# A planner's places, open pairs and initial copies in the projections of a pre-LN transformer block, and the last attention unit's projection in whole rows

## The chip, the cores and the metric

One NeuronCore of a Trainium2 chip runs the whole program; nothing is shared with other cores. The metric is device microseconds of one execution. Engines are named as in the profile: PE is TensorE's matmuls, PEld its weight loads, DVE is VectorE, ACT is ScalarE, POOL is GpSimd, and SP is the engine whose queue issues nearly all DMAs.

## The reference

A sequential block with 2048 tokens of width 640: layer norm without scale, 32-head attention with heads of 20, a residual, layer norm again, a SwiGLU feed-forward of width 1728, a residual.

```python
def _A_ref(x, wqkv, wo):                      # H = 32, Dh = 20
    qkv = transpose((x @ wqkv).reshape(B, S, 3, H, Dh), (2, 0, 3, 1, 4))
    q, k, v = qkv[0], qkv[1], qkv[2]
    p = softmax(einsum("bhqd,bhkd->bhqk", q, k) * Dh ** -0.5)
    o = einsum("bhqk,bhkd->bhqd", p, v)
    return transpose(o, (0, 2, 1, 3)).reshape(B, S, D) @ wo
def _B_ref(x, w_gate, w_up, w_down):
    return (silu(x @ w_gate) * (x @ w_up)) @ w_down
h = x + _A_ref(layernorm(x), wqkv, wo)
return h + _B_ref(layernorm(h), w_gate, w_up, w_down)
```

All in fp32. The kernel keeps the accuracy by splitting an operand into a high part and a rest and adding three products.

## The kernel before

**Stages.** First the projections to queries, keys and values for four chunks of 512 tokens (`query_key`, `value`). Then the attention in 32 units (eight groups of four heads, four query chunks each), each of 16 steps `kt` over 128 keys. Last the output projection, the second norm and the feed-forward; part of the output projection lies inside the last units.

**Two halves of TensorE.** In the projections each product uses 64 of the 128 rows of the array. A job (15 products on the lower half, then 15 on the upper) runs its upper half beside the next job's lower half. `Halves` plans this while the program is written: `t` is the modelled time of each half, `free` that of each engine, `places` the modelled release of each PSUM bank, and `now()`, `use`, `stream` and `wait` move them. The instructions' order on every engine comes out of this model; at run time each engine works through its queue in order and waits on semaphores.

**Pairs.** The softmax needs each query row's maximum over the keys. Part of these maxima is found in the projections, between their products. A *pair* of key blocks is handled as max(a, b) = a + relu(b − a): POOL forms b − a (line 431), one product of the queries with the differences goes through a ReLU on ScalarE into an SBUF place, and a second product with a is added to the place and reduced to a maximum by VectorE, which then releases the place. `max_twice` (lines 217, 231 and 224) does this for one half and leaves the second product as a closure: the pair is *open* until `finish_second` issues it. `max_differences` (lines 194, 205 and 207) does it for both halves at once. `pair` decides whether a pair starts now. There are three places (`relus`: two halves of `spare`, and `third_relu`, given up near the end), and `next_place` hands them out in turn. Before the change at most one pair a half is open:

```python
if half is None and any(self.second) or half is not None and self.second[half]:
    return False
```

**What pairs read.** Keys and queries are written to DRAM by `keep` and loaded back by `stack` (line 161 on SP) into tiles that are free at that time: quarters of `k_stk`, four `raw` tiles in which the weights had arrived, later parts of `xt` and `z_lo`. `raw_place` first copies 1024 finite elements a partition into such a `raw` tile, since POOL's differences run over all 128 rows of it: one copy at job 6, three at job 9 (line 379). `queries_at` is the time from which the planner takes the first units' queries (loaded back the same way) as there.

**Transposes.** The next chunk's normalized tokens are transposed by TensorE in `flip` (line 783), which takes two banks and is copied out by ScalarE (line 791).

**The last units.** A step of a unit issues four scores (line 1374, then the exponential on ScalarE, line 1380) and the weighing of an earlier step's probabilities with the values (`weigh`, line 1384, four matmuls). In the last unit two steps' weighings stand together at even steps and none at odd ones, until `kt` 14 (`both`). Beside them stand the output projection of a chunk (`project`, line 1103: 15 matmuls a product, two products a 128-token tile, eight in all), one a step in steps 0 to 7, and the transposes of its normalized rows (line 1135) in steps 12 to 15. With `halved` a product is split into 30 matmuls of 64 rows in two banks, which VectorE adds one after the other (line 1109); only the projection of chunk 1, inside the last unit, is halved.

Of the kernel before, what the change touches and what calls it, by code (L numbers as in the profile page):

```python
# [13 lines left out]
AF = mybir.ActivationFunctionType  # L14
# [10 lines left out]
NT = S // P  # L25
CH = 512
# [12 lines left out]

LEAST = -3.0e38  # L40
MARGIN = 0.2
BEHIND = 2
SHARE = 4
LAST_QUARTER = 60
# [5 lines left out]
def tile_block(ctx: ExitStack, tc: tile.TileContext, x, wqkv, wo, wg, wu, wd, out):  # L50
# [287 lines left out]
    with tc.tile_pool(name="pa", bufs=2) as pa:  # L338
# [30 lines left out]
        def raw_tile():  # L369
            return pa.tile([P, ND, 2 * P], F32R, name="raw", bufs=4)  # L370

        def raw_place():
            return place(raw_tile().rearrange("p a b -> p (a b)")[:, : 2 * CH], nc.scalar)

        def place(t, engine=nc.sync):

            if engine is nc.scalar:
                some = w_hi.rearrange("p k c -> p (k c)")[:, : 2 * CH].bitcast(F32)
                nc.scalar.activation(t, some, AF.Copy)
                pe.use("scalar", 1.0)  # L380
                return t.rearrange("p (h n) -> p h n", h=2)
            for b in range(2):
                some = w_hi[b * ROW + NPART : (b + 1) * ROW].rearrange("r k c -> r (k c)")[:, : 2 * CH]
                rows = t[b * ROW + NPART : (b + 1) * ROW]
                nc.sync.dma_start(rows.bitcast(F32), some.bitcast(F32))
            pe.sp(n=2, kb=32)
            return t.rearrange("p (h n) -> p h n", h=2)
# [56 lines left out]
        def staged_keys(u, kc, ks, q=None, since=0):  # L444

            ns = ks if q is None else [*ks, q]
            if len(ks) == 2:
                all_products = [
                    (t, pair, b) for t in range(TPC) for pair in range(2) for b in range(2)
                ]  # L450
            else:
                all_products = [(t, pair, None) for t in range(TPC) for pair in range(2)]

            def one(t, pair, b, at):
                rows = queries[u] if q is None else items[q][3]
                if b is None:
                    max_differences(mxs[u], rows, items[ks[0]][3], pair, t, kc, next_place(), at)
                    return over()
                first, more = (items[k][3] for k in ks)
                second = max_twice(mxs[u], rows, first, more, pair, t, kc, b, next_place(), at)  # L460
# [18 lines left out]
            return [  # L479
                (  # L480
                    lambda: slot[0] >= since and all(map(there, ns))
                    and (q is not None or pe.now() >= queries_at.get(u, math.inf)),
                    lambda at, a=a: one(*a, at), a[2],
                )
                for a in all_products
            ]
# [28 lines left out]
        third_relu = v_stk[0].rearrange("p t w -> p (t w)")[:, 2 * CH :]  # L515
        relus.append(third_relu)

        def next_place():
            relus.append(relus.pop(0))
            return relus[-1]  # L520

        def next_pair():
            load_items()
# [6 lines left out]
        class Halves:  # L530
# [5 lines left out]
            def __init__(self):  # L536
                self.t = [0.0, 0.0]
                self.free = dict.fromkeys(("vector", "scalar", "pool", "sync", "dma"), 0.0)
                self.places = dict.fromkeys(range(8), 0.0)
                self.second = [None, None]  # L540
                self.last = 0.0
                self.jobs = []

# [61 lines left out]
            def pair(self):  # L605
                t = self.now()
                if not self.banks(1):
                    return False
                queue = next_pair()
                if queue is None:  # L610
                    return False
                least = int(self.t[1] < self.t[0])
                ahead = 0
                if queue[0][2] == 1 - least and len(queue) > 1 and queue[1][2] == least:
                    ahead = int(queue[1][0]())
                half = queue[ahead][2]
                if half is None and any(self.second) or half is not None and self.second[half]:
                    return False
                at = self.banks(1 if half is not None else 2)
                if at is None:  # L620
                    return False
                second = queue.pop(ahead)[1](at)
                if half is not None:
                    start = self.stream(half, 0.231)
                    seen = self.use("scalar", 0.48, start + 0.43) + 0.2
                    self.places[at[0]] = seen
                    self.second[half] = second, seen
                    return True
                for half in range(2):
                    self.stream(half, 0.231)  # L630
                ends = [t + 0.43] * 2
                ends = [self.use("scalar", 0.3, end) + 0.2 for end in ends]
                for i, end in zip(at, ends):
                    self.places[i] = self.use("vector", 0.36, end) + 0.14
                return True

            def before_flip(self):
# [33 lines left out]
            def finish_second(self, half):  # L671
                if not self.second[half]:
                    return False
                second, seen = self.second[half]
                at = self.banks(1)
                if at is None or self.now() + 0.43 < seen:
                    return False
                self.second[half] = None
                second(at)
                start = self.stream(half, 0.231)  # L680
                self.places[at[0]] = self.use("vector", 0.62, max(seen, start + 0.43)) + 0.14
                return True

            def wait(self, us):
# [148 lines left out]
        def keep(c, m, ps):  # L833

            e = next_e()
            start = max(pe.now() + 0.4, e_free.get(id(e), 0.0))
            if slot[0] < 8:
                done = pe.use("scalar", 0.5, start)
                free = ready = pe.use("vector", 0.62, done + 0.2)
                split(ps, e[:, 0], e[:, 1], nc.vector)  # L840
            else:
                free = pe.use("scalar", 0.5, start)
                done = pe.use("scalar", 0.5)
                engine, ready = pe.second_part(done + 0.2)
# [12 lines left out]
            store(e, ready + 0.2, *pieces)  # L857
            return free
# [73 lines left out]
        for at, (kind, c, *which) in enumerate(work):  # L932
# [55 lines left out]
            for u, when in enumerate((5, begins(1) + 14, begins(2) + 14)):  # L988
                if at == when - 4:
                    es[:] = [e for e in es if all(e is not stored(q) for q in lent[:u])]  # L990
                if at == when:
                    assert landed[0, 0, u] == GD
                    load_queries(u)
                    queries_at[u] = pe.sp(n=4, kb=750) + 3.5
            if 0 in ends:
                finish_at = min(finish_at, at + 2)
                if at == finish_at:
# [457 lines left out]
    for u in range(NU):  # L1455
# [4 lines left out]
        for kt in range(NT):  # L1460
# [5 lines left out]
            for op in order:  # L1466
# [2 lines left out]
                elif op in "sS":  # L1469
                    scores(u, kt, heads[op == "S"].pop(0), probs)  # L1470
                else:
                    both = u == NU - 1 and kt < NT - 1
                    for _ in range(2 * (1 - kt % 2) if both else 1):
                        if todo:
                            weigh_next()
# [58 lines left out]
    def ps_b():  # L1534
        return banks[:, turn(one_places)]
# [554 lines left out]
```

## Time and profile before

| | us |
|---|---|
| median of three runs (lowest, highest) | 2037.76 (2036.97, 2040.04) |
| the profiled execution | 2040.81 |
| its span, first to last instruction | 2039.0 |
| projections, from the start to the first scores | 335 |
| attention up to the last unit | 1089 |
| last unit of the attention | 53 |
| the rest | 563 |

The mean granted TensorE clock is 0.996 of full speed. In the lines of the profile a row of a timeline has the start, the busy time, the engine, the line, the operation with what it writes and reads, the count, and in brackets the idle time of the engine ahead of it with what ended it. A row of a window has its bounds, its length, the busy time and count of PE, PEld, DVE, ACT and POOL, the granted clock, the DMA share and GB/s. Matmuls overlap, so their busy times add to more than the distance of their starts.

### The profile page before, as it was taken

How to read it: one execution, taken by the hardware profiler on the slowest of the kernel's cores; microseconds unless marked ns; L12 is line 12 of the kernel's file. 1: busy time of each engine (PE TensorE's matmuls, PEld its weight loads, DVE VectorE, ACT ScalarE, POOL GpSimd, SP SyncE). 2: the span in 40 equal slices, each digit the busy share in tenths (PEclk: the TensorE clock that was granted, in tenths of full speed). 3: DMA queues.
4: the chain of work that ended last, by engine and by line, in shares of the span. 5: the costliest groups of instructions: out<-in, count | busy, mean ns of one | idle time of the engine just before them, and what ended most of it. 6: DMA issues, size and time to landing. Idle time of an engine off the chain costs nothing.

```text
span 2039.0 us, 39356 instructions
## 1 busy us (share of the span) xinstructions
PE 2009.1 (99%) x13836; PEld 1244.3 (61%) x13836; DVE 1616.7 (79%) x3261; ACT 1463.3 (72%) x2948; POOL 778.5 (38%) x1075
## 2 busy tenths in 40 slices
PE   7999999999999999999999999999999999999998
PEld 6888897333333333333333333345598888888888
DVE  7769776888888888888888888886478666676677
ACT  4887887999999999999999999996634222212221
POOL 4464342234343434344430011001146454754555
PEclk9999999999999999999999999999999999999999
DMA  7775574343533534444433123211159654974642
GB/s 228 236 214 184 167 215 116 104 137 103 150 125 108 158 112 143 135 145 137 149 127 108 30 61 83 82 62 49 36 180 325 208 193 154 350 267 158 204 149 92
DMA packets 205206, 304.93 MB, mean 150 GB/s; under 512 B 47648, under 2 KB 82720, under 8 KB 203984
## 3 DMA queue, kind: packets, MB, share of 16 engines
q1 hardware_dynamic: 204912, 302.40, 45.6%
q8 instruction: 110, 1.80, 0.4%
q14 instruction: 88, 0.72, 0.1%
q10 hardware_dynamic: 96, 0.00, 0.0%
HBM read 205.78 MB, written 95.68 MB: 148 GB/s over the span
## 4 chain that ended last, share of the span: by engine, by line
PE 94%; DMA 2%; DVE 1%; ACT 1%; POOL 1%; issue 1%; SPq 0%; DVEq 0%; ACTq 0%; POOLq 0%
PE banks L1384 25%; PE banks L1374 17%; PE banks L1552 16%; PE banks L238 12%; PE banks L1646 8%; PE banks L569 8%; PE banks L1103 3%; PE banks L217 3%; PE banks L194 1%; DMA qk_d<-e 0%; PE banks L826 0%; PE banks L263 0%; DMA q_stk<-qk_d 0%; ACT q_stk L231 0%; DMA xt<-in_A_x 0%
## 5 line engine op out<-in xcount | busy, mean ns | idle before, releaser
L1380 ACT ACTIVATE probs<-banks 128x512 f32<-128x512 f32 x2048 | 1056.2, 614 | 61.1 <-PE banks L1374 25.3
L244 DVE TENSOR_REDUCE mx<-banks 128x1 f32<-128x512 f32 x1472 | 925.4, 684 | 124.9 <-PE banks L238 76.3
L1374 PE MATMUL banks<-q_stk,k_stk 62*128 62x512 f32 x2048 | 583.2, 428 | 1.5 <-ACT probs L1380 1.5
L1384 PE MATMUL banks<-probs,v_stk 128*32 128x512 f32 x4096 | 545.4, 606 | 0.0
L238 PE MATMUL banks<-k_stk,q_stk 60*128 60x512 f32 x1472 | 486.7, 438 | 0.2
L1374 PEld LDWEIGHTS banks<-q_stk,k_stk 62*128 62x128 f32 x2048 | 291.8, 184 | 283.7 <-ACT probs L1380 271.4
L238 PEld LDWEIGHTS banks<-k_stk,q_stk 60*128 60x128 f32 x1472 | 244.2, 184 | 163.1 <-DVE mx L244 126.8
L1769 DVE TENSOR_TENSOR tmp<-banks,tmp 128x512 f32<-128x512 f32 x208 | 141.2, 689 | 118.4 <-PE banks L1552 92.8
L1384 PEld LDWEIGHTS banks<-probs,v_stk 128*32 128x32 f32 x4096 | 81.3, 108 | 183.1 <-issue 171.4
L1646 PE MATMUL banks<-halves,yp 128*128 128x320 f32 x1032 | 178.9, 308 | 1.4 <-POOL yp L97 1.2
L1646 PEld LDWEIGHTS banks<-halves,yp 128*128 128x128 f32 x1032 | 165.2, 188 | 17.4 <-POOL yp L97 1.5
L1552 PE MATMUL banks<-t,units 128*128 128x512 f32 x624 | 162.7, 396 | 0.1
L97 POOL TENSOR_TENSOR yp<-y,yp 128x256 fp32r<-128x256 f32 x96 | 60.3, 628 | 195.2 <-ACT yp L96 181.0
L1552 PE MATMUL banks<-z,units 128*128 128x512 f32 x516 | 133.8, 394 | 0.0
L255 POOL CAST both<-neg 128x16 fp32r<-128x16 f32 x32 | 6.6, 206 | 314.7 <-PE banks L1374 138.2
L1552 PEld LDWEIGHTS banks<-t,units 128*128 128x128 f32 x624 | 112.5, 188 | 18.9 <-DVE tmp L1769 0.3
L1651 DVE TENSOR_TENSOR h<-banks,h 128x320 f32<-128x320 f32 x248 | 110.0, 481 | 6.8 <-PE banks L1646 5.4
L224 DVE CUSTOM_DVE_ANT_0 q_stk<-banks,q_stk 128x512 f32<-128x512 f32 x139 | 92.7, 687 | 26.0 <-PE banks L217 13.2
L569 PE MATMUL banks<-z_hi,w_hi 64*128 64x512 f32 x380 | 102.4, 406 | 1.9 <-ACT z_hi L96 1.8
L569 PE MATMUL banks<-z_lo,w_hi 64*128 64x512 f32 x380 | 103.3, 395 | 0.0
L1552 PEld LDWEIGHTS banks<-z,units 128*128 128x128 f32 x516 | 93.1, 187 | 16.1 <-DVE tmp L1769 0.2
L96 ACT ACTIVATE yp<-tmp 128x512 fp32r<-128x512 f32 x40 | 25.3, 632 | 103.2 <-POOL tmp L1639 103.2
(213 smaller groups left out, 2960.9 us busy)
## 6 DMA issues: line engine op xcount, KB each, us to landing
units<-w_d SPq DMA_DIRECT2D x186, 256.0 KB
w_d<-stage SPq DMA_DIRECT2D x106, 256.0 KB
halves<-j_d SPq DMA_DIRECT2D x70, 320.0 KB
k_stk<-qk_d SPq DMA_DIRECT2D x116, 160.0 KB
j_d<-stage SPq DMA_DIRECT2D x42, 320.0 KB
q_stk<-qk_d SPq DMA_DIRECT2D x64, 160.0 KB
k_stk<-qk_d SPq DMA_DIRECT2D x116, 80.0 KB
rb<-r_d SPq DMA_DIRECT2D x32, 256.0 KB
```

Of the source, the lines that this page charges most:

```text
L217: nc.tensor.matmul(ps, q[rows, pair, t * P : (t + 1) * P], k[rows, pair, :], start=True, stop=True)
L224: nc.vector.tensor_tensor_reduce(out=place, in0=ps, in1=place, scale=1.0, scalar=LEAST, op0=ALU.add, op1=ALU.max, accum_out=mx[:, b, pair, ...
L238: nc.tensor.matmul(ps, queries[u][rows, pair, t * P : (t + 1) * P], keys[u // NC][rows, pair, kc * CH : (kc + 1) * CH], start=True, stop=True,
L244: nc.vector.tensor_reduce(mxs[u][:, b, pair, t, kc : kc + 1], ps, axis=AX.X, op=ALU.max)
L569: product = nc.tensor.matmul(job["ps"][:, :out], lhs, rhs, start=(half == 0 and i == 0), stop=(half == 1 and i == job["n"] - 1),)
L1374: nc.tensor.matmul(ps, keys[u // NC][rows, p, kt * P : (kt + 1) * P], queries[u][rows, p, :], start=True, stop=True,)
L1380: nc.scalar.activation(probs[p][:, b, :], ps, AF.Exp, scale=scale)
L1384: nc.tensor.matmul(acc[32 * j : 32 * j + 32, :], values[u // NC][:, kt, j * VW : j * VW + 32], probs[j // 2][:, j % 2, :], start=(kt == 0) ...
L1552: nc.tensor.matmul(ps.rearrange("p (t n) -> p t n", t=TPC), w[k][:, i], z[k][:, :, j], start=(first and m == 0), stop=(last and m == len(n ...
L1646: nc.tensor.matmul(ps, a, b, start=(n == 0), stop=(n == len(pairs) - 1))
L1651: nc.vector.tensor_tensor(out=h, in0=ps, in1=h, op=ALU.add)
L1769: add = lambda out, ps, x: nc.vector.tensor_tensor(out=out, in0=ps, in1=x, op=ALU.add)
```

## The change

Seven edits. In the planner: a pair's place is the one with the earliest modelled release (`relu_at`), and a pair starts only if that lies before its ReLU could begin (`free_place`); up to two pairs a half are open (`OPEN`). The initial copies of the `raw` tiles go from ScalarE to VectorE, and `place_at` keeps such a tile unused until the copy's modelled end. In `keep` the modelled times of two ScalarE steps go from 0.5 to 0.62 and 0.54 us. The allowance for the first queries' landing goes from 3.5 to 4.5 us. In the last unit the weighings stand in twos only until `kt` 9. No projection is halved any more.

```diff
+OPEN = 2
-            if engine is nc.scalar:
+            if engine is nc.vector:
                 some = w_hi.rearrange("p k c -> p (k c)")[:, : 2 * CH].bitcast(F32)
-                nc.scalar.activation(t, some, AF.Copy)
-                pe.use("scalar", 1.0)
-                return t.rearrange("p (h n) -> p h n", h=2)
+                nc.vector.tensor_copy(t, some)
+                t = t.rearrange("p (h n) -> p h n", h=2)
+                place_at[id(t)] = pe.use("vector", 0.65) + 0.2
+                return t
...
-        def next_place():
-            relus.append(relus.pop(0))
-            return relus[-1]
+        relu_at = {}
+        def free_place(at):
+            place = min(relus, key=lambda r: relu_at.get(id(r), 0.0))
+            return place if relu_at.get(id(place), 0.0) <= at else None
...
-                if half is None and any(self.second) or half is not None and self.second[half]:
+                if half is None and any(self.second) or half is not None and len(self.second[half]) == OPEN:
                     return False
                 at = self.banks(1 if half is not None else 2)
                 if at is None:
                     return False
-                second = queue.pop(ahead)[1](at)
+                place = free_place(t + 0.43)
+                if place is None:
+                    return False
+                second = queue.pop(ahead)[1](at, place)
+                relu_at[id(place)] = math.inf
...
-                    self.second[half] = second, seen
+                    self.second[half].append((second, seen, place))
...
+                relu_at[id(place)] = self.places[at[1]]          # pair
...
-                self.second[half] = None
+                del self.second[half][0]
                 second(at)
                 start = self.stream(half, 0.231)
                 self.places[at[0]] = self.use("vector", 0.62, max(seen, start + 0.43)) + 0.14
+                relu_at[id(place)] = self.places[at[0]]          # finish_second
...
-                free = pe.use("scalar", 0.5, start)
-                done = pe.use("scalar", 0.5)
+                free = pe.use("scalar", 0.62, start)
+                done = pe.use("scalar", 0.54)
...
-                    queries_at[u] = pe.sp(n=4, kb=750) + 3.5
+                    queries_at[u] = pe.sp(n=4, kb=750) + 4.5
...
-                    both = u == NU - 1 and kt < NT - 1
+                    both = u == NU - 1 and kt < NT // 2 + 2
...
                     ahead = projection(
-                        c - 1, ps_max if c < NC - 1 else (lambda: ps_b()), c == NC - 2
+                        c - 1, ps_max if c < NC - 1 else (lambda: ps_b())
                     )
```

The order of the instructions changes from the first pair on. Line numbers of the new program are 1 to 10 higher (569 is 573, 194 is 195, 783 is 793, 1374 is 1384, 1384 is 1394, 1103 is 1113, 1135 is 1145).

TensorE at the first pair of the projections (L783 is the first transpose, L569 a projection's product, L194 the first pair's two products). Before:

```order
L783 MATMUL banks<-ident,xt 128x64 x8
L569 MATMUL banks<-z_lo,w_hi 128x512
L194 MATMUL banks<-k_stk_116,q_stk 128x512 x2
L569 MATMUL banks<-z_hi,w_hi 128x512
L569 MATMUL banks<-z_lo,w_hi 128x512
```

Now:

```order
L793 MATMUL banks<-ident,xt 128x64 x8
L573 MATMUL banks<-z_lo,w_hi 128x512
L573 MATMUL banks<-z_hi,w_hi 128x512
L573 MATMUL banks<-z_lo,w_hi 128x512
L573 MATMUL banks<-z_hi,w_hi 128x512
L573 MATMUL banks<-z_lo,w_hi 128x512
L573 MATMUL banks<-z_hi,w_hi 128x512
L573 MATMUL banks<-z_lo,w_hi 128x512
L573 MATMUL banks<-z_hi,w_hi 128x512
L573 MATMUL banks<-z_lo,w_hi 128x512
L195 MATMUL banks<-k_stk_116,q_stk 128x512 x2
```

Eight more products of a projection stand ahead of the first pair.

ScalarE around the three copies of job 9 before (L791 and L96 belong to a transpose, L205 are ReLUs of pairs):

```order
L791 ACTIVATE xt<-banks 128x4x64 x2
L96 ACTIVATE z_hi<-xt 128x512
L379 ACTIVATE raw<-w_hi 128x1024 x3
L205 ACTIVATE v_stk_117<-banks 128x256 x2
L205 ACTIVATE q_stk<-banks 128x256 x4
```

VectorE there now (ISA is the reduction of a pair with its accumulator read, L98 a rest of a split):

```order
L208 ISA v_stk_117,mx_121<-banks,v_stk_117 128x256
L208 ISA mx_121 128x1
L380 CAST raw<-w_hi 128x1024 x3
L98 TENSOR_TENSOR v_stk_117<-v_stk_117 128x512
L208 ISA q_stk,mx_121<-banks,q_stk 128x256
```

The copies left ScalarE's queue ahead of the ReLUs and stand in VectorE's between two pairs' reductions.

TensorE in the last unit from step 11 on (L1374 scores, L1384 weighings of four matmuls a step, L1135 transposes, L1103 the projection that follows). Before:

```order
L1374 MATMUL banks<-q_stk,k_stk_4721 128x512 x8
L1384 MATMUL banks<-probs,v_stk_4722 32x512 x8
L1135 MATMUL banks<-ident,z_17209 128x128 x5
L1374 MATMUL banks<-q_stk,k_stk_4721 128x512 x4
L1135 MATMUL banks<-ident,z_17239 128x128 x5
L1374 MATMUL banks<-q_stk,k_stk_4721 128x512 x4
L1384 MATMUL banks<-probs,v_stk_4722 32x512 x8
L1135 MATMUL banks<-ident,z_17264 128x128 x5
L1374 MATMUL banks<-q_stk,k_stk_4721 128x512 x4
L1384 MATMUL banks<-probs,v_stk_4722 32x512 x4
L1135 MATMUL banks<-ident,z_17293 128x128 x5
L1384 MATMUL banks<-probs,v_stk_4722 32x512 x4
```

Now, from step 13 on:

```order
L1394 MATMUL banks<-probs,v_stk_4722 32x512 x4
L1145 MATMUL banks<-ident,z_17107 128x128 x5
L1384 MATMUL banks<-q_stk,k_stk_4721 128x512 x4
L1394 MATMUL banks<-probs,v_stk_4722 32x512 x4
L1145 MATMUL banks<-ident,z_17136 128x128 x5
L1384 MATMUL banks<-q_stk,k_stk_4721 128x512 x4
L1394 MATMUL banks<-probs,v_stk_4722 32x512 x4
L1145 MATMUL banks<-ident,z_17161 128x128 x5
L1394 MATMUL banks<-probs,v_stk_4722 32x512 x8
L1113 MATMUL banks<-wo_hi,o_hi 128x320 x5
```

Each step now has its scores, one weighing and one transpose, and two weighings in place of one stand at the end.

More of the change, by code (lines that the diff above doesn't have):

```diff
@@ L372, in raw_place @@
         def raw_place():
[L373 removed]
+            return place(raw_tile().rearrange("p a b -> p (a b)")[:, : 2 * CH], nc.vector)
         def place(t, engine=nc.sync):
[L377 removed]
+            if engine is nc.vector:
                 some = w_hi.rearrange("p k c -> p (k c)")[:, : 2 * CH].bitcast(F32)
[L379 to L381 removed]
+                nc.vector.tensor_copy(t, some)
+                t = t.rearrange("p (h n) -> p h n", h=2)
+                place_at[id(t)] = pe.use("vector", 0.65) + 0.2
+                return t
             for b in range(2):
@@ L452, in staged_keys, with one @@
                 all_products = [(t, pair, None) for t in range(TPC) for pair in range(2)]
-            def one(t, pair, b, at):
+            def one(t, pair, b, at, place):
                 rows = queries[u] if q is None else items[q][3]
                 if b is None:
-                    max_differences(mxs[u], rows, items[ks[0]][3], pair, t, kc, next_place(), at)
+                    max_differences(mxs[u], rows, items[ks[0]][3], pair, t, kc, place, at)
                     return over()
                 first, more = (items[k][3] for k in ks)
-                second = max_twice(mxs[u], rows, first, more, pair, t, kc, b, next_place(), at)
+                second = max_twice(mxs[u], rows, first, more, pair, t, kc, b, place, at)
                 return lambda at: (second(at), over())
@@ L482, in staged_keys @@
                     and (q is not None or pe.now() >= queries_at.get(u, math.inf)),
-                    lambda at, a=a: one(*a, at), a[2],
+                    lambda at, place, a=a: one(*a, at, place), a[2],
                 )
@@ L539, in __init__ @@
                 self.places = dict.fromkeys(range(8), 0.0)
-                self.second = [None, None]
+                self.second = [], []
                 self.last = 0.0
@@ L673, in finish_second @@
                     return False
-                second, seen = self.second[half]
+                second, seen, place = self.second[half][0]
                 at = self.banks(1)
```

## The prediction

> **What bounds the kernel now.** I read the page first, then the stages, then TensorE's waits in the stages that the change touches.
>
> ```profile
> PE 2009.1 (99%) x13836; PEld 1244.3 (61%) x13836; DVE 1616.7 (79%) x3261; ACT 1463.3 (72%) x2948; POOL 778.5 (38%) x1075
> PE 94%; DMA 2%; DVE 1%; ACT 1%; POOL 1%; issue 1%; SPq 0%; DVEq 0%; ACTq 0%; POOLq 0%
> 0.00:335.00 335.00, 314.30 (x2856) 289.05 (x2857) 246.81 (x864) 252.19 (x545) 150.33 (x126) 0.98 0.66 204
> 1423.80:1476.40 52.60, 51.55 (x453) 31.09 (x449) 23.66 (x59) 34.97 (x68) 7.51 (x5) 0.97 0.12 35
> ```
>
> The first line is the busy time of each engine, the second the chain that ended last by engine, and the other two are stages: length, then busy time of PE, PEld, DVE, ACT and POOL, the granted clock, the DMA share and GB/s. TensorE is the chain, so the time moves only if its idle time, its clock or its own work moves. The change touches two stages. The projections (0 to 335 us) keep TensorE busy 314.3 of 335 us at a clock of 0.98. The last unit of the attention (1423.8 to 1476.4 us) is its end.
>
> What TensorE waits for between 17 and 335 us (waiter, releaser, us, times, longest), and below it two waits of ACT that lie behind the largest of them:
>
> ```profile
> PE banks L217 <- ACT q_stk L231: 4.3, 5, 1.6
> PE banks L783 <- DVE mx L207: 1.7, 1, 1.7
> PE banks L194 <- DMA q_stk<-qk_d: 1.3, 2, 1.0
> PE banks L217 <- ACT v_stk L231: 1.2, 1, 1.2
> PE banks L194 <- DMA raw<-qk_d: 0.5, 1, 0.5
> PE banks L783 <- ACT q_stk L231: 0.4, 1, 0.4
> ...
> ACT q_stk L231 <- DVE mx L224: 7.0, 6, 2.0
> ACT v_stk L231 <- DVE mx L224: 2.0, 2, 1.3
> ```
>
> A pair product waits because its bank still waits for ScalarE's ReLU. That ReLU waits because the place it writes is still being read by VectorE's reduction. This is 4.3 + 1.2 + 0.4 = 5.9 us of TensorE, from 9.0 us of ScalarE.
>
> A wait costs more than itself. The granted clock stood at half in four stretches (the seventh column of figures, 0.50):
>
> ```profile
> 46.94:50.35 3.41, 3.41 (x18) 3.09 (x20) 2.75 (x9) 1.99 (x6) 0.58 (x1) 0.50 0.59 179
> 60.59:64.00 3.41, 3.37 (x23) 3.28 (x25) 1.57 (x9) 3.35 (x10) 1.65 (x2) 0.50 0.59 210
> 173.23:176.64 3.41, 3.41 (x20) 3.16 (x18) 3.04 (x13) 1.72 (x4) 0.00 (x0) 0.50 0.31 118
> 1463.47:1466.88 3.41, 3.41 (x20) 1.12 (x13) 0.00 (x0) 1.56 (x3) 1.54 (x1) 0.50 0.02 5
> ```
>
> Each lasts 3.41 us and does half the work, so it costs 1.7 us; three stand behind a wait in the projections and one in the last unit. The Trainium skill, "TensorE: Matmul & The Clock Gate", Part 1, says that TensorE's clock is halved after an idle window of about 3.4 us on a free-running grid. The length agrees with these rows; the windows ahead of them were not wholly idle, so here a part of a window is enough.
>
> **The change part by part.** The profiled execution took 2040.8 us (span 2039.0), 3.0 us above the median 2037.8 of the three runs. The sum is made against 2040.8, and its difference is then taken from the median.
>
> *First pair (the queries' allowance 3.5 to 4.5).* In the new order nine products of a projection stand ahead of the first pair, where one stood.
>
> ```profile
> 26.26 1.29 PE L569 MATMUL banks<-z_lo,w_hi 64*128 64x512 f32 x5
> 28.98 0.98 PE L569 MATMUL banks<-z_hi,w_lo 64*128 64x512 f32 x6
> 29.66 0.39 PE L569 MATMUL banks<-z_lo,w_hi 64*128 64x512 f32 x1
> 46.00 0.47 PE L194 MATMUL banks<-k_stk,q_stk 60*128 60x512 f32 x1 [1.03 <-DMA q_stk<-qk_d]
> 46.79 0.63 PE L194 MATMUL banks<-k_stk,q_stk 60*128 60x512 f32 x1 [0.32 <-DMA q_stk<-qk_d]
> ```
>
> One product takes 0.39 us; six that alternate between the halves take 0.98, so they start (0.98 − 0.39) / 5 = 0.12 us apart; five of one half take 1.29, so 0.23 apart. Eight products earlier fill 8 × 0.12 = 0.9 us of the wait, which the landings (46.00 and 46.79) set and which doesn't move. The half-clock stretch at 46.94 then has a busier window ahead; I give its going 0.7. Term: −0.9 − 0.7 × 1.7 = −2.1 us (0 to −2.6).
>
> *Initial copies into the four places, ScalarE to VectorE.*
>
> ```profile
> 56.56 2.93 ACT L379 ACTIVATE raw<-w_hi 128x1024 fp32r<-128x1024 f32 x3
> 59.79 0.42 DVE L207 CUSTOM_DVE_ANT_0 v_stk<-banks,v_stk 128x256 f32<-128x256 f32 x1 [5.30 <-ACT v_stk L205]
> L755 DVE TENSOR_SCALAR xt<-xt,mv,r_a x8: 605/610/1587, 11.1 to 41.7; 128x640 f32<-128x640 f32 x8
> 52.32 0.42 DVE L207 CUSTOM_DVE_ANT_0 v_stk<-banks,v_stk 128x256 f32<-128x256 f32 x1 [2.31 <-ACT v_stk L205]
> ```
>
> Three copies hold ScalarE for 2.93 us; VectorE sits idle 5.30 us behind them, and TensorE's transposes (L783) 1.65 us behind VectorE, then run at half clock. With the copies on VectorE, ScalarE's ReLUs start 2.9 us earlier. No row shows such a copy on VectorE; the nearest one-operand row does 640 elements in 0.605 to 1.587 us, so 1024 cost some 0.6 us at least and 2.5 at most, 2 to 7.5 us for the three. I take about 1 each, near the median row. Cover: VectorE's idle 2.31 and 5.30 us at that place. Without cover they delay three pairs' reductions, and the 1.65 us stays. The fourth, at about 38 us, stands ahead of the normalization that feeds the first transposes; what it delays is made up by the wait for the queries behind. Term: −0.8 × (1.65 + 1.7) = −2.7 us (0 to −3.4).
>
> *Places by modelled release, two open pairs a half.* A pair now starts only when a place is free in the model, so part of the 9.0 us of ScalarE's waits becomes projection products put ahead. But the model's release is no measurement, and the place is taken as soon as it says so. I take a third of 5.9 + 1.7 = 7.6 us, −2.5 (0 to −7.6, and the other sign as a rival). Against it, pairs bunch on one half: counted over the order by operand rows, products that follow one of their own half rise from 474 to 514. Each gives up at most 0.23 − 0.12 = 0.11 us: 40 × 0.11 = 4.4 us if TensorE would otherwise not have waited. I take +3.0 (0 to +4.4), since most of the stage is not waiting. In the new order the last pairs stand at the end of the projections, not some jobs ahead of it; their loads move with them on SP, and POOL's differences behind those. Apart from the queries TensorE waited for such a load once, 0.5 us; I take 0, and 2 at most, four such waits. The allowances of 0.62 and 0.54 us issue nothing: 0.
>
> *Weighing in the last unit (paired until step 10, not 15).*
>
> ```profile
> L1380 ACT ACTIVATE probs<-banks 128x512 f32<-128x512 f32 x32 | 16.2, 622 | 6.5 <-PE banks L1374 5.8 <-PE banks L1103 0.8
> 1467.65 4.03 ACT L1380 ACTIVATE probs<-banks 128x512 f32<-128x512 f32 x8 [2.62 <-PE banks L1374]
> 1458.01 1.92 PE L1384 MATMUL banks<-probs,v_stk 128*32 128x512 f32 x16
> 1459.86 0.73 PE L1374 MATMUL banks<-q_stk,k_stk 62*128 62x512 f32 x4
> 1473.41 1.06 PE L1384 MATMUL banks<-probs,v_stk 128*32 128x512 f32 x8
> 1474.41 0.77 PE L1135 MATMUL banks<-ident,z 128*128 128x128 f32 x5
> 1476.38 1.00 PE L1103 MATMUL banks<-wo_hi,o_hi 128*128 128x320 f32 x5
> ```
>
> The first row is ScalarE between 1452 and 1476.4 us: eight steps of exponentials, 16.2 / 8 = 2.03 us a step, and 5.8 us idle until scores. A double weighing holds TensorE 1.85 us (1458.01 to 1459.86) ahead of the next scores, with a flip 2.6 us, more than ScalarE's 2.03. A single one holds it 1.0 us, with a flip (0.77) 1.8, so ScalarE is then nearly fed. I leave 1.5 us of the 5.8 for the four flips, whose banks VectorE must empty, and 1.0 us for the one weighing that now comes behind the last exponential: −(5.8 − 1.5 − 1.0) = −3.3 us (−0.5 to −4.8). The half-clock stretch at 1463 lies inside these 5.8 us and isn't counted again. What follows at 1476.38 is TensorE's own work, so the gain stays.
>
> *Whole rows for the second projection (eight products of 15 matmuls).*
>
> ```profile
> 1366.27 1.00 PE L1103 MATMUL banks<-wo_hi,o_hi 128*128 128x320 f32 x5
> 1367.10 0.90 PE L1103 MATMUL banks<-wo_lo,o_hi 128*128 128x320 f32 x5
> 1367.84 0.90 PE L1103 MATMUL banks<-wo_hi,o_lo 128*128 128x320 f32 x5
> 1368.66 0.50 PE L1374 MATMUL banks<-q_stk,k_stk 62*128 62x512 f32 x1
> 1423.88 1.03 PE L1103 MATMUL banks<-wo_hi,o_hi 64*128 64x320 f32 x10
> 1426.20 0.63 PE L1374 MATMUL banks<-q_stk,k_stk 62*128 62x512 f32 x4
> L1103 PEld LDWEIGHTS banks<-wo_lo,o_hi 128*128 128x128 f32 x120 | 18.6, 188 | 0.0
> ```
>
> Whole rows take 1368.66 − 1366.27 = 2.39 us, halves 1426.20 − 1423.88 = 2.32. Eight times 0.07 is +0.6; half of VectorE's adds for it go, off the path. I take +0.3 (−0.6 to +2.5, the upper end if the scores beside it no longer slip in between the halves). The same page of the Trainium skill, Part 3, "The mechanism", says that weight loads overlap running matmuls only in other row groups, which speaks against whole rows. The trace disagrees: five whole products start within 0.74 us (1367.10 to 1367.84), 0.15 each, less than a load's 0.188. By that rule the sum would be the last rival's.
>
> Sum: −2.1 − 2.7 − 2.5 + 3.0 − 3.3 + 0.3 = −7.3 us: 2033.5 us for an execution like the profiled one, 2030.5 for the median.
>
> **The rivals.** *The modelled release is too early (slower).* VectorE's row of 0.605 to 1.587 us shows that equal work varies by 1 us, and the norm's steps sit in front of the reductions. With two pairs open, ScalarE meets an unreleased place more often; all behind it in its queue (the evictions, the flips' copies) waits too, and then TensorE. If the eight waits become sixteen, TensorE pays another 5.9 us and two more half-clock stretches, 3.4: −2.1 − 2.7 + 3.0 − 3.3 + 0.3 + 9.3 = +4.5, or 2042.3 us. It ends above today's time from about fifteen waits on. For it: no slack is added to the modelled release. Against it: the before had no check at all. 0.16.
>
> *The waits only move (no change).* The queries still land at 46.79, the half-clock stretches come back at other places, the flips in the last unit wait for VectorE: −0.9 for the first pair, −1.65 for the transposes, +3.0, −1.0 in the last unit, 0 elsewhere: −0.5, or 2037.3 us. Also the case in which three places keep two open pairs from ever mattering. 0.16.
>
> *Whole rows expose their loads (slower).* 8 × 15 × 0.188 = 22.6 us: −7.6 + 22.6 = +15, or 2052.8 us. The rows above speak against it. 0.03.
>
> **How the numbers follow.** The forecast has 0.65; its own range is 2024 to 2036 us. Best ends of all terms: −2.6 − 3.4 − 7.6 + 0 − 4.8 − 0.6 = −19; unlikely together. The range reaches from 2022 to 2042.5: it takes in the no-change case and the first rival, and leaves out some 0.07 below and 0.1 above. A measurement of this kernel tells about 0.2% (4.1 us) from no change, so faster means under 2033.7 and slower over 2041.8. Faster 0.62 (nearly all of the forecast's 0.65); same 0.20 (the rest of it, the no-change case and the milder first rival); slower 0.18.
>
> **What would show it.** Right: no L783 wait for a reduction near 60 us; no half clock in the first 65 us; ScalarE's waits for mx reductions below 6 us; projections ending some 4 us earlier than 335 us; ScalarE's idle time ahead of exponentials in the last eight steps near 2 us. Wrong: TensorE's waits for ReLUs at 6 us or more, or copies on VectorE over 2 us with the transposes still waiting. Projection products slower than 2.5 us in the last unit would refute the whole-rows term.

## The result and the profile after

The changed kernel took 2030.6 us (median of 8 runs, 2027.9 to 2034.9), the kernel before 2038.6 us (median of 8, 2034.7 to 2040.1): ratio 0.9965, 95% interval 0.9953 to 0.9976, so 8 us or 0.35% faster. The forecast was 2030.5 us. The sum came out; most of its terms, as the experiments show, did not, so that the match is luck.

The profiled execution of the changed kernel took 2031.8 us with a span of 2030.0, 9.0 us less than the one before. Its page, busy time by engine and the chain that ended last:

```profile
PE 2004.5 (99%) x13716; PEld 1237.3 (61%) x13716; DVE 1622.2 (80%) x3257; ACT 1459.9 (72%) x2944; POOL 777.7 (38%) x1075
...
PE 91%; DMA 3%; DVE 2%; POOL 1%; ACT 1%; issue 1%; SPq 0%; ACTq 0%; POOLq 0%; DVEq 0%
```

TensorE is still the bound. The same stages as before (busy time of PE, PEld, DVE, ACT, POOL; the granted clock is the column after POOL's), and the one half-clock stretch that is left before the end:

```profile
0.00:327.90 327.90, 311.08 (x2856) 284.10 (x2857) 254.44 (x868) 248.76 (x541) 148.57 (x126) 1.00 0.67 208
1416.70:1467.50 50.80, 50.35 (x333) 28.47 (x329) 20.55 (x52) 35.00 (x68) 7.56 (x5) 0.97 0.12 35
1452.50:1455.91 3.41, 3.41 (x16) 0.85 (x12) 0.00 (x0) 2.80 (x6) 0.00 (x0) 0.50 0.00 0
```

The projections end 7.1 us earlier (327.9 against 335.0 us, with the same 2856 matmuls), at clock 1.00 in place of 0.98: the three half-clock stretches, 3 x 1.7 = 5.1 us, are absent, TensorE's waits below are 4.1 us shorter (7.9 against 12.0), and what is left, TensorE's own work in its new order, is 2.0 us longer. From there to the last unit the two traces run in step, 7.1 us apart. The last unit is 1.8 us shorter, with one half-clock stretch in it as before.

TensorE's waits between 17 and 320 us (us, times, longest), and below them ScalarE's for reductions:

```profile
PE banks L573 <- ACT z_hi L97: 2.1, 2, 1.2
PE banks L573 <- DVE mx L225: 1.2, 1, 1.2
PE banks L218 <- ACT e L352: 1.1, 1, 1.1
PE banks L218 <- DVE mx L225: 0.8, 1, 0.8
PE banks L836 <- ACT z_hi L97: 0.8, 1, 0.8
PE banks L793 <- DVE mx L208: 0.7, 1, 0.7
PE banks L573 <- DVE mx L208: 0.5, 1, 0.5
PE banks L793 <- DVE xt L765: 0.5, 1, 0.5
PE banks L573 <- ACT ev L883: 0.2, 1, 0.2
...
ACT q_stk L232 <- DVE mx L225: 3.9, 6, 2.2
ACT v_stk L232 <- DVE mx L225: 2.7, 3, 1.7
ACT q_stk L206 <- DVE mx L225: 0.5, 1, 0.5
```

The rows of before that had a ReLU as releaser (L217 and L783 behind L231, 5.9 us) are all gone. ScalarE still waits 7.1 us for reductions, in ten places, against 9.0 in eight, but no row of TensorE's has a ReLU behind such a wait as its releaser any more.

### The profile page after: what moved, and what is told of

It is laid out like the page before. It is cut to its first block, busy times and chain, and to the rows that moved or that the text cites. A ratio compares the mean times of both kernels' runs of the same rounds, so it can differ in the third digit from the quotient of the medians.

```text
span 2030.0 us, 39123 instructions
## 1 busy us (share of the span) xinstructions
PE 2004.5 (99%) x13716; PEld 1237.3 (61%) x13716; DVE 1622.2 (80%) x3257; ACT 1459.9 (72%) x2944; POOL 777.7 (38%) x1075
## 3 DMA queue, kind: packets, MB, share of 16 engines
q8 instruction: 109, 1.79, 0.4%
## 4 chain that ended last, share of the span: by engine, by line
PE 91%; DMA 3%; DVE 2%; POOL 1%; ACT 1%; issue 1%; SPq 0%; ACTq 0%; POOLq 0%; DVEq 0%
PE banks L1394 25%; PE banks L1384 17%; PE banks L1562 16%; PE banks L239 11%; PE banks L1656 8%; PE banks L573 6%; PE banks L1113 4%; PE banks L218 2%; DMA k_stk<-qk_d 1%; PE banks L195 1%; DMA raw<-qk_d 1%; DMA qk_d<-e 1%; PE banks L836 0%; DMA qk_d<-q_stk 0%; DMA v_d<-ev 0%
## 5 line engine op out<-in xcount | busy, mean ns | idle before, releaser
L1390 ACT ACTIVATE probs<-banks 128x512 f32<-128x512 f32 x2048 | 1056.3, 612 | 59.0 <-PE banks L1384 22.6
L1384 PE MATMUL banks<-q_stk,k_stk 62*128 62x512 f32 x2048 | 581.3, 430 | 1.1 <-ACT probs L1390 1.1
L1384 PEld LDWEIGHTS banks<-q_stk,k_stk 62*128 62x128 f32 x2048 | 290.6, 185 | 284.8 <-ACT probs L1390 271.1
L98 POOL TENSOR_TENSOR yp<-y,yp 128x256 fp32r<-128x256 f32 x96 | 60.4, 630 | 195.1 <-ACT yp L97 180.8
L573 PE MATMUL banks<-z_hi,w_lo 64*128 64x512 f32 x380 | 102.0, 391 | 0.0
```

Source lines behind the costliest of these rows:

```text
L573: product = nc.tensor.matmul(job["ps"][:, :out], lhs, rhs, start=(half == 0 and i == 0), stop=(half == 1 and i == job["n"] - 1),)
L1384: nc.tensor.matmul(ps, keys[u // NC][rows, p, kt * P : (kt + 1) * P], queries[u][rows, p, :], start=True, stop=True,)
L1390: nc.scalar.activation(probs[p][:, b, :], ps, AF.Exp, scale=scale)
```

## The experiments

Each was timed in five rounds beside the kernel before; the ratios below are to that. Line numbers are those of the kernel that is changed, give or take one.

**The projections' edits without the last unit's** (from the changed kernel):

```diff
-                    both = u == NU - 1 and kt < NT // 2 + 2
+                    both = u == NU - 1 and kt < NT - 1
...
-                        c - 1, ps_max if c < NC - 1 else (lambda: ps_b())
+                        c - 1, ps_max if c < NC - 1 else (lambda: ps_b()), c == NC - 2
```

> The changed kernel with its two edits in the last unit undone: weighing paired until step 15 and the second projection in halves again, as before; the whole change of the projections stays. By the prediction's terms the projections give -2.1 - 2.7 - 2.5 + 3.0 = -4.3 us (ratio 0.998). Theory from the two traces: the projections end 7.1 us earlier (327.6 against 334.8 us), the three half-clock stretches there (5.1 us) being gone, so -7 us (0.9965). Rival: the whole change comes from the last unit and the profiled projections were a lucky execution: 0 to -2 us.

Measured: 2031.4 us, 0.9961 (0.9947 to 0.9975), as the changed kernel within the intervals. The projections carry the change; their end lies at 326.8 us. The two edits of the last unit add nothing here that the times can tell.

**The weighing alone** (kernel before, `kt < NT // 2 + 2`):

> The kernel before, with the weighing paired until step 10 as the only edit. Prediction: -3.3 us (ratio 0.9984), ScalarE's idle time ahead of exponentials in the last eight steps from 5.8 to some 2 us. Rival: the flips then wait for VectorE, -1.0 us (0.9995). Projections and halves as before: no row outside the last eight steps moves.

Measured: 2035.4 us, 0.9976 (0.9966 to 0.9986), -2.9 to -6.9 us. From the score of step 505 (of 512) to the last weighing it needs 18.4 us, the kernel before 20.9, each with one half-clock stretch there: -2.6 us. Over the other profiles, without a stretch it is 19.3 us paired and 17.3 us single (-2.0). ScalarE's idle time until scores in the last eight steps is 2.4 us in this run, as priced (5.8 before). In the changed kernel, between 1444.5 and 1467.5 us, it is 3.1 us:

```profile
ACT probs L1390 <- PE banks L1384: 3.1, 5, 1.0
```

**Whole rows alone** (kernel before, without `c == NC - 2`):

> The kernel before, with whole rows for the second projection as the only edit. Prediction: +0.3 us (ratio 1.000). Theory from the trace after: two steps of the last unit take 7.98 us in place of 7.75 while the projection runs, four times 0.23, so +0.9 us (1.0005). Rival, weight loads exposed: +15 us (1.007).

Measured: 2039.4 us, 1.0001 (0.9991 to 1.0011): no difference that can be told. Steps 496 to 505 show it nevertheless: 33.8 to 33.9 us in every profile with whole rows, 33.0 in every one with halves, so +0.9. Where it lies is seen in TensorE's timeline (start, length), first before, then after:

```profile
1433.22 0.90 PE L1103 MATMUL banks<-wo_hi,o_lo 64*128 64x320 f32 x10
1433.96 0.63 PE L1374 MATMUL banks<-q_stk,k_stk 62*128 62x512 f32 x4
1434.43 0.46 PE L1103 MATMUL banks<-wo_hi,o_hi 64*128 64x320 f32 x2
```

```profile
1424.72 1.00 PE L1113 MATMUL banks<-wo_hi,o_hi 128*128 128x320 f32 x5
1425.56 0.90 PE L1113 MATMUL banks<-wo_lo,o_hi 128*128 128x320 f32 x5
1426.30 0.90 PE L1113 MATMUL banks<-wo_hi,o_lo 128*128 128x320 f32 x5
1427.12 0.74 PE L1384 MATMUL banks<-q_stk,k_stk 62*128 62x512 f32 x4
1427.79 1.00 PE L1113 MATMUL banks<-wo_hi,o_hi 128*128 128x320 f32 x5
```

The product itself takes 2.40 us (1424.72 to 1427.12), as priced. The four scores behind it cost 0.67 us from start to next start, beside halves 0.47. This meeting comes once in two steps, so four times 0.2, or 0.8 of the 0.9.

**The copies alone** (kernel before, the four copies on VectorE with their price and `place_at`):

> The kernel before, with the four copies on VectorE (priced 0.65 us each in the model, with the time at which the place may be loaded) as the only edit. Prediction: -2.7 us (ratio 0.9987): no wait of a transpose near 60 us, no half-clock stretch behind it. Rival (waits only move): -1.65 us and a half-clock stretch elsewhere, 0 net. The model's prices change, so the order behind the copies changes too; if that order alone matters, the difference may have either sign by 2 us with waits at other places.

Measured: 2043.2 us, 1.0021 (1.0011 to 1.0031): slower. No transpose waits near 60 us and no half-clock stretch lies in the projections, and still they end at 334.6 us. TensorE's waits for ReLUs stand in the new order as in the old:

```profile
PE banks L217 <- ACT q_stk L231: 4.5, 4, 1.4
PE banks L217 <- ACT v_stk L231: 0.6, 1, 0.6
```

**The places undone** (changed kernel; the places in turn, one open pair):

```diff
-            place = min(relus, key=lambda r: relu_at.get(id(r), 0.0))
-            return place if relu_at.get(id(place), 0.0) <= at else None
+            relus.append(relus.pop(0))
+            return relus[-1]
```

> The changed kernel with the part on the places undone: the three places are taken in turn again whatever their release, one open pair a half; all other edits stay. Theory (the release is what removes the waits): TensorE's waits for ReLUs that wait for a reduction, 0 in the changed kernel, come back to 4 to 6 us, with one or two half-clock stretches of 1.7: +5 to +8 us on the changed kernel, 2036 to 2039 us. TensorE's order taken alone (each product as long as its columns, halves side by side) is as long as that of the changed kernel (299.0 against 299.1 us), so the order says 0. Rival (the changed kernel's order is a lucky one and the release does nothing): 2031 us, or any value within 4 us, with no such waits.

Measured: 2036.4 us, 0.9980 (0.9971 to 0.9989). The projections end at 333.4 us, 5.7 later than in the changed kernel, and these waits come back, 6.2 us:

```profile
PE banks L218 <- ACT v_stk L232: 2.9, 2, 1.6
PE banks L218 <- ACT q_stk L232: 2.4, 4, 1.1
PE banks L793 <- ACT q_stk L232: 0.9, 2, 0.6
```

**One open pair a half** (changed kernel, `OPEN = 1`):

> The changed kernel with one open pair a half in place of two; places by modelled release as in the change. Theory: the release alone keeps ReLUs from waiting, and with one open pair fewer products follow one of their own half (490 against 514; TensorE's order taken alone is 297.1 against 299.1 us): -2 us on the changed kernel, 2028.5 us, waits for ReLUs still 0. Rival (the second open pair is what gives the planner enough pairs to put in): pairs fall behind, +2 us or more, 2033 us.

Measured: 2032.4 us, 0.9959 (0.9944 to 0.9973), as the changed kernel within the intervals. The waits are lower still (4.6 us, none for ReLUs), but the pairs fall behind: the projections' last product stands at 317.3 us, and pairs are left with nothing beside them. A half-clock stretch of three times 3.41 us stands there, which costs 5.1 us. The run before this one differs from it only in how a place is chosen: without the check on the release it took 4.0 us more, with 6.2 us of waits for ReLUs against none. The half clock:

```profile
322.79:333.03 10.24, 10.02 (x36) 5.55 (x39) 7.56 (x30) 8.47 (x21) 7.01 (x2) 0.50 0.18 50
```

**Copies back on ScalarE** (changed kernel):

> The changed kernel with the four copies on ScalarE again. Prediction's term: +2.7 us, 2033.3 us, with a transpose waiting for a reduction near 55 to 60 us by 1.5 us and a half-clock stretch behind it in most executions. Rival (the copies alone made the kernel before slower by 4 us, so their move costs): -2 us or more, 2028 us.

Measured: 2030.0 us, 0.9948 (0.9933 to 0.9962): not slower, and not clear of the changed kernel's interval. The transposes wait 0.3 us, for an eviction, and a product 0.9 us for a reduction; the half-clock stretch did come, at 56.69 us.

**The queries' allowance back at 3.5** (changed kernel):

> The changed kernel with the queries' allowance of 3.5 again. Prediction's term: +2.1 us, 2032.7 us, the first pair waiting 1 us for its queries near 46 us and a half-clock stretch there. TensorE's order taken alone is 1.0 us longer, which would make it +3. Rival (the window of the clock lies elsewhere): +0.9 us, 2031.5 us, no half-clock stretch before 65 us.

Measured: 2027.8 us, 0.9938 (0.9924 to 0.9952): faster. The first pair does wait for its queries again (start, length, idle before), but 45.70 to 49.10 us has the full clock. One more row of this run is shown, a pair product that waits for a ReLU; that ReLU had waited for no reduction, it stood in a queue in which ScalarE worked without a gap from 51.56 us on:

```profile
45.75 0.46 PE L195 MATMUL banks<-k_stk,q_stk 60*128 60x512 f32 x1 [0.68 <-DMA q_stk<-qk_d]
```

```profile
PE banks L195 <- ACT q_stk L206: 0.6, 1, 0.6
```

```profile
45.70:49.10 3.40, 3.35 (x30) 3.30 (x32) 2.29 (x6) 3.29 (x8) 1.30 (x2) 1.00 0.57 186
```

**The places alone** (kernel before with `free_place`, `relu_at` and two open pairs a half, nothing else):

> The kernel before, with the places by modelled release and two open pairs a half as the only edits (allowance of the queries, copies, ScalarE's prices and the last unit as before). Theory (the release removes TensorE's waits for ReLUs): L218's waits for ReLUs, 5.5 us before, go to 0, with one half-clock stretch or two: -6 to -9 us, ratio 0.9957 to 0.997. TensorE's order taken alone is 0.6 us longer (296.9 against 296.3). Prediction's terms for this part: -2.5 + 3.0 = +0.5 us (1.0002). Rival (orders differ by luck): any value within 4 us, and waits for ReLUs left.

Measured: 2030.3 us, 0.9955 (0.9939 to 0.9972). This one part gives what the whole change gives. In its profile the projections end 10.7 us earlier than before: 6.7 us of waits, 3.4 of two half-clock stretches, 0.6 of the rest. TensorE's waits between 17 and 320 us are four rows, none behind a ReLU, with the transposes' wait of before (1.7 us, and a half-clock stretch behind it at 59.3 us) still there:

```profile
PE banks L572 <- ACT z_hi L97: 1.7, 2, 1.1
PE banks L792 <- DVE mx L208: 1.7, 1, 1.7
PE banks L572 <- DVE mx L208: 1.2, 1, 1.2
PE banks L572 <- DVE mx L225: 0.7, 1, 0.7
```

**The changed kernel without the allowance and with halves**, and **the same with the copies on ScalarE too**:

> The changed kernel with the queries' allowance of 3.5 and the halved second projection again: the run with the allowance alone put back took 2027.8 us (ratio 0.9938), and whole rows cost 0.23 us in each of four pairs of steps, so 0.9 less: 2026.9 us, 0.9934. Rival (the faster run came of its chip, not of the order): 2030.5 us, 0.996.

> As the kernel with the allowance and the halves put back, and the four copies on ScalarE too: what stays of the change is the places, ScalarE's two prices and the weighing. If parts add up: the copies put back alone gave 0.0017 less than the changed kernel, so 0.9917. Rival (parts don't add, each edit to the planner's numbers gives another order): 0.992 to 0.997, a transpose waiting for a reduction near 55 us again.

Measured: 2027.3 us, 0.9941 (0.9927 to 0.9954), and 2029.7 us, 0.9954 (0.9939 to 0.9969). The first has the projections in the same order as the run with the allowance alone put back, on another chip, so that the rival falls. The sum of the parts, 0.9917, lies outside the second's interval, so the parts do not seem to add. But the copies put back moved the ratio by -0.0017 in one order and by +0.0013 in the other, each within the intervals; in the other a transpose waits 1.6 us for a reduction again.

**A place given out 0.3 us after its modelled release** (changed kernel):

```diff
-            return place if relu_at.get(id(place), 0.0) <= at else None
+            return place if relu_at.get(id(place), 0.0) <= at - 0.3 else None
```

> The changed kernel, with each place given out 0.3 us after its modelled release. The prediction's first rival says that the release is modelled too early; then ScalarE's waits for reductions (7.1 us in the changed kernel) fall below 3 us and the time falls by 1 to 2 us. Theory (these waits no longer reach TensorE): 0 from the waits, and +2 us from the order, whose length taken alone is 301.3 against 299.1 us, so 2032 us, 0.997.

Measured: 2026.0 us, 0.9936 (0.9921 to 0.9950), the lowest median of all, ahead of the changed kernel (0.9953 to 0.9976) with intervals that don't meet, though the two were run beside different executions of the kernel before. ScalarE's waits for reductions fall from 7.1 to 2.4 us, and TensorE's are:

```profile
PE banks L573 <- ACT z_hi L97: 1.3, 2, 0.8
PE banks L793 <- DVE mx L208: 0.7, 1, 0.7
PE banks L218 <- DVE mx L225: 0.3, 1, 0.3
PE banks L573 <- ACT ev L883: 0.2, 1, 0.2
```

All runs side by side. The end is the start of the last product of the projections. Waits are the sums of TensorE's rows between 17 and 320 us, "ReLU" those of pair products and transposes behind a ReLU; stretches are the half-clock ones before the projections' end; the last column is the end less the waits and 1.7 us a stretch.

| kernel | ratio | end of projections | stretches | waits | ReLU | rest |
|---|---|---|---|---|---|---|
| before | 1 | 334.8 | 3 | 12.0 | 5.9 | 317.7 |
| weighing alone | 0.9976 | 334.1 | 2 | 11.6 | 5.0 | 319.1 |
| whole rows alone | 1.0001 | 334.7 | 3 | 11.1 | 4.9 | 318.5 |
| copies alone | 1.0021 | 334.6 | 0 | 8.6 | 5.3 | 326.0 |
| places undone | 0.9980 | 333.4 | 1 | 9.0 | 6.2 | 322.7 |
| changed | 0.9965 | 327.6 | 0 | 7.9 | 0 | 319.7 |
| projections' edits only | 0.9961 | 326.8 | 0 | 6.8 | 0 | 320.0 |
| places alone | 0.9955 | 324.1 | 1 | 5.3 | 0 | 317.1 |
| copies back | 0.9948 | 326.9 | 1 | 8.1 | 0 | 317.1 |
| allowance back | 0.9938 | 324.0 | 0 | 5.4 | 0.6 | 318.6 |
| allowance, halves back | 0.9941 | 324.1 | 0 | 5.3 | 0 | 318.8 |
| allowance, copies, halves back | 0.9954 | 327.3 | 0 | 7.9 | 0 | 319.4 |
| release 0.3 us later | 0.9936 | 320.1 | 0 | 2.5 | 0 | 317.6 |

(One open pair is left out, since its pairs end after the projections.) With the modelled release TensorE has no wait for a ReLU in six of seven different orders of the projections (one open pair among them), and in the seventh the 0.6 us shown above, for a ReLU that had not waited for a reduction. Without it every kernel has 4.9 to 6.2 us, in three orders. Where the rest is 317 to 320 us, the waits and stretches say nearly by themselves when the projections end. The rest is not exact: it holds the time to the first product, which starts at 23.6 us in the changed kernel, at 24.9 in the run with the projections' edits only, whose projections have the same order, and at 22.2 with the later release, so 1.4 us of that run's earlier end arise ahead of the first pair.

## Why the prediction came out, by its own steps

**Places by modelled release: right mechanism, mis-sized, and the main term.** The prediction took a third of 7.6 us, -2.5; all of the waits for ReLUs went. The places alone gave 0.9955, -6 to -12 us.

**Bunching on one half, +3.0: too much, and not settled.** The two profiles with the changed order (514 products behind one of their own half) have rests of 319.7 and 320.0 us, the three with the order of before (474) have 317.7 to 319.1: some 1.4 us more on average, as much as two profiles of one order differ. And the count does not set the rest: the later release has 518 and 317.6, the places alone 480 and 317.1. TensorE's order taken alone said that the later release costs 2 us, and it had the lowest time, so an order's length without its waits did not rank these kernels. Together the two terms stood at +0.5 us where the part alone measured -9. The step that failed is the third of the waits: all of them went.

**First pair, -2.1: wrong as a gain.** The wait for the queries went, as said (no row has it in the changed kernel). Yet with the allowance back the kernel was faster by 0.0027 (the intervals just miss each other), and the same order of the projections gave 0.9941 once more. The term gave 0.7 x 1.7 us to a half-clock stretch that is not tied to this wait (below), and took the rest of the order as unmoved.

**Copies, -2.7: wrong as a gain.** Their price was near: three took 3.00 us on VectorE, one each, as estimated. But a transpose still waits for a reduction, at 55.86 us:

```profile
55.86 0.81 PE L793 MATMUL banks<-ident,xt 64*128 64x64 f32 x8 [0.73 <-DVE mx L208]
```

Put in alone they cost 0.0021; put back in the changed kernel they cost nothing that can be told (-0.0017, within the intervals). The prediction priced the place at 60 us and not the reordering of everything behind it. Why the copies alone end with a rest of 326.0 us, 8 above the kernel before's, no run settles; it stays open, as does the 322.7 of the places undone. These two orders have 528 and 516 products behind one of their own half, the copies alone the most of all, so bunching is a candidate that was not tried apart.

**Weighing, -3.3: right way, somewhat large.** It is -2.0 us without a half-clock stretch, -2.6 with one, -2.9 to -6.9 by the times of whole runs, in which paired weighing also met two stretches at times (22.6 us from step 505 in two profiles). **Whole rows, +0.3: right sign, +0.9** by the steps, by the cause that the upper end named, scores that no longer slip in between halves. Weight loads were not exposed.

So most of the 8 us came from the places, with the allowance giving part back. The last unit adds 1.1 to 1.7 us in the traces (weighing less whole rows), which whole times do not show (0.9965 with its edits, 0.9961 without). The forecast sum was met by errors that cancel, which is luck: the places, with bunching, stood some 9 us too high in it, and 4.8 us of gain were put down to the first pair, which cost time, and to the copies, which gained none.

**The rivals.** *Release too early* was right in part: ScalarE's waits stayed at 7.1 us, above the 6 that the prediction set, and 0.3 us of slack took them to 2.4 and the time down. No row shows them reach TensorE directly. Through ScalarE's queue, the way that the rival names, some may: with allowance, copies and halves back, ScalarE worked without a gap from a ReLU at 225.05 us, which had waited 0.84 us for a reduction, to the step at 227.86 for which a product then waited 0.9 us. It made none of these kernels slower than the kernel before. *The waits only move* holds for single edits (copies alone), not for the whole. Of the signs to look for, "no half clock in the first 65 us" came true and shows nothing, since all three kernels with the allowance put back had none there either.

## What to carry to other kernels

Where a planner orders the work, a change to one of its prices reorders all that follows: cost the mechanism by the waits it can remove over the stage, not by the one place in the trace that it was written for, and try it alone. A check that keeps work from being put in ahead of its buffer's release is such a mechanism, since it held in all seven orders here; an allowance, put in for one place, is not. A total that agrees proves none of its terms.

## What the runs showed of the hardware

*Half-clock stretches move between executions.* The weighing-alone kernel has the same instructions in the same order as the kernel before up to the last unit. Its clock (the column after POOL's) in the two stretches that the prediction priced, and in the two it had instead:

```profile
46.94:50.35 3.41, 3.41 (x34) 3.27 (x32) 2.87 (x10) 3.02 (x9) 1.83 (x2) 1.00 0.66 191
60.59:64.00 3.41, 3.41 (x40) 3.07 (x37) 2.15 (x12) 3.35 (x11) 3.41 (x3) 1.00 0.71 220
99.12:102.53 3.41, 3.41 (x22) 3.21 (x24) 2.27 (x14) 0.72 (x3) 3.41 (x3) 0.50 0.76 227
174.22:177.63 3.41, 3.41 (x18) 2.71 (x18) 2.12 (x8) 1.63 (x3) 0.00 (x0) 0.50 0.32 120
```

A wait is followed by half clock in one execution and not in the next, so a stretch in one profile is a chance and not a price. Within an execution the stretches start whole multiples of 3.41 us apart (in the kernel before 60.59 - 46.94 = 13.65, four of them; here 174.22 - 99.12 = 75.10, twenty-two), but from one execution to the other they do not (99.12 - 46.94 = 52.18, or 15.3). Averaged over runs, as an estimate from the mean granted clocks, the clock lost (1 - 0.9975) x 2039 = 5.1 us in the kernel before (27 runs) and (1 - 0.9989) x 2031 = 2.3 in the changed one (8 runs): some 3 of the 8 us. The Trainium skill, "TensorE: Matmul & The Clock Gate", Part 1, has the window free-running, with a run-variable phase; these rows agree.

*VectorE's copies meet GpSimd.* Of the four copies three took 0.69 us at most, one 1.79:

```profile
L380 DVE CAST raw<-w_hi x4: 685/688/1789, 40.3 to 52.0; 128x1024 fp32r<-128x1024 f32 x4
```

```profile
51.87 1.34 POOL L98 TENSOR_TENSOR z_lo<-xt,z_hi 128x512 fp32r<-128x512 f32 x1 [2.03 <-ACT z_hi L97]
53.18 1.73 POOL L433 TENSOR_TENSOR k_stk<-k_stk 128x512 fp32r<-128x512 f32 x1
```

The long one began at 52.0 us, behind GpSimd's subtraction of 51.87, and ended about 0.6 us after that one did (53.21). In the run with the places undone the same subtraction began at 53.32 us, as the last copy ended, and no copy was long:

```profile
L380 DVE CAST raw<-w_hi x4: 684/686/690, 41.4 to 52.7; 128x1024 fp32r<-128x1024 f32 x4
```

The Trainium skill, "SBUF — State Buffer", "Who interferes with whom", says that a VectorE cast in a two-port mode and a GpSimd instruction lock each other out, the later one waiting wholly; these rows agree, though none shows the mode. Whether this also moved the pairs' reductions was not tried apart.
